# Asking for an expert's rows ahead of its weights, its gates later, and 144 idle products behind the last one

## The chip, the core and the metric

The kernel runs on one core of one Trainium2 chip. The metric is the device time of one execution in microseconds. Before the change it is 754.23 us (median of three runs, 753.93 to 754.88).

The engines as the profile names them: PE is TensorE's matmul side and PEld its weight loads, DVE is VectorE, ACT is ScalarE, POOL is GpSimd, SP issues most of the DMAs.

## The reference: attention within hash buckets, then a mixture of experts

The inputs are q, k and v of shape (4, 8, 768, 64), a projection to 6 bits, a router `w_gate` of 512 x 8 and eight experts with `w1` (512 x 1024) and `w2` (1024 x 512), all fp32. Cut to what matters:

```python
mask = q_bucket[:, :, :, None] == k_bucket[:, :, None, :]
scores = np.where(mask, scale * np.matmul(q, k.transpose(0, 1, 3, 2)), -1e9)
attn = np.exp(scores - np.max(scores, axis=-1, keepdims=True))
attn = attn / (np.sum(attn, axis=-1, keepdims=True) + 1e-09)
x = np.matmul(attn, v)                       # to (3072, 512): all heads of a token
expert_idx = np.argmax(x @ w_gate, axis=1)   # one expert a token
for e in range(E):                           # over the rows sorted by expert
    y_sorted[lo:hi] = np.maximum(x_sorted[lo:hi] @ w1[e], 0.0) @ w2[e]
out = gate_w[:, None] * y                    # rows back in their places
```

## The kernel before

**Two halves.** Up to about 450 us the attention runs over 16 pairs of heads (one batch element each four), by an order that is written out by hand. Each finished token is scattered by POOL to `sorted_rows` in DRAM: a row of 578 numbers, with its 512 features (in four pieces, each between router logits), its gate value and its token number, at a slot of its expert. Then the experts run, the most loaded first: the ranks are computed on the chip and the expert numbers read into SP's registers.

**Phases.** `PH` lists the phases: 0 and 1 are the first 256 rows and the rest of the rank-0 expert, phase n from 2 on is the expert of rank n - 1, with at most `CAPS[n - 1]` rows (512, 456, 432, ..., 354). Rows above the cap would go through a loop at the end (line 1100), which is branched around when there are none.

**Products in three parts.** An fp32 operand is split into a rounded part (fp32r) and the rest; a product is the sum of three fp32r products. So a weight goes through ACT, which copies the rounded part (L624), and POOL, which subtracts it (L625). A phase has two stages on PE: `mm1` (L729) makes eight feature blocks, 12 products each, and each block is emptied from PSUM by ACT (`relu` "u", L743) and then DVE (the rest, "d", L745); then `mm2` makes the output, for phases of at most 384 rows token by token (L786, 24 products a tile), otherwise feature by feature (L766) with transposes (L795) in the next phase. The PSUM tiles named `s` rotate over three buffers, so the fourth use of one waits for the eviction of the first. DVE scales a finished tile by its gates (L797), POOL scatters it to the output (L799).

**Weights.** A rank has four chunks: chunk 4r and 4r + 1 are the column halves of `w1`, 4r + 2 and 4r + 3 the row halves of `w2`. `raw_load(c, a)` (L611) asks for half a of chunk c, 512 KB, into rotating buffers; `chunk_part(c, i)` does a quarter of the conversion. `halves` (called after each feature block) converts a quarter and asks for a half that comes some chunks later. The buffer of a half is free when POOL has done its last quarter, and SP waits for that in its queue.

**Rows.** `rows(n)` asks SP for the rows of phase n: from phase 2 on four loads of 32-row blocks (`xb`, L641, one for each 128 features) and one small load with gate and token number (`xg`, L646). `xt_blocks(n)` later copies gate and token (L675, L657), transposes the blocks on DVE (L679) and splits them (ACT L680, DVE L682) into `xh`, which `mm1(n)` multiplies. It is called between the `mm2` tiles of phase n - 1.

**Queues.** Each engine runs its instructions in the order of the program. On ACT the conversions (L624) stand between the evictions (L743): behind feature block f stands quarter f % 4 of the next chunk, so a conversion whose weights aren't there holds back the evictions behind it. SP's DMAs all go through one queue (q1). `rows(2)` stands at the start of phase 1, behind `raw_load(4, 0)`, `raw_load(4, 1)` and `raw_load(5, 0)`.

**The end.** The last 98 rows of the last phase are made in two column halves (`youts`, L819): DVE empties the first, ACT the second (L823), POOL scatters each (L826). Then each engine branches around the loop for spilled rows (L1099) and meets the others in a barrier (L1159), ahead of which SP waits until the last output has landed.

## Time and profile before

| | before |
|---|---|
| runs | 754.23 us median (753.93 to 754.88) |
| profiled execution | 755.68 us, span 753.9 us |
| PE busy | 745.7 us (99% of the span), 4723 products |
| ACT, POOL, DVE busy | 483.2, 470.5, 456.5 us |
| DMA | 113.71 MB, 151 GB/s on average |
| phase 1 on PE | from 470.15 us (L729), its `mm2` from 481.78 us |
| phase 2 on PE | from 494.01 us |
| last product ends | 748.97 us |

In the rows of the profile a group stands as line, engine, operation, output <- input by the program's names, shapes and count; a bracket at the end of a timeline row gives the idle time of the engine ahead of it and what ended it. In a row of waits stand the total, the number and the longest, in us. "DMA to landing" is the time from a DMA's issue to its completion. An fp32 product that isn't a transpose shows as two products with a weight load each.

### The profile page before, as it was taken

The numbers are of one execution on the slowest core, as the hardware profiler recorded it, in microseconds if no ns is written. First come the engines' busy times: TensorE is split into PE (matmuls) and PEld (weight loads), VectorE is DVE, ScalarE is ACT, GpSimd is POOL, SyncE is SP. The second block draws the span as 40 slices with busy tenths as digits, with TensorE's granted clock in tenths as the row PEclk, the third lists the DMA queues.
The fourth block names the chain that finished last, engine by engine and source line by source line (L and its number), as shares of the span: only waits on it lengthen the run. The fifth ranks groups of instructions, "written<-read, shape, count | busy, mean of one in ns | idle before, by whom it ended". The sixth has DMA issues, their size and how long they took to land.

```text
span 753.9 us, 13381 instructions
## 1 busy us (share of the span) xinstructions
PE 745.7 (99%) x4723; PEld 616.2 (82%) x4723; DVE 456.5 (61%) x1042; ACT 483.2 (64%) x942; POOL 470.5 (62%) x575
## 2 busy tenths in 40 slices
PE   9999999999999999999999999999999999999997
PEld 5778777777787787877778788889999999989896
DVE  7766766767676676676688775254383925262421
ACT  7879878878887887887887761464344444453410
POOL 6867355578635768735766643576666666668532
PEclk9999999999999999999999999999999999999999
DMA  8499844235325335422343323956636476736401
GB/s 283 168 315 277 280 128 168 83 133 193 128 64 168 121 111 200 154 75 67 101 173 116 116 73 134 253 160 189 155 135 170 144 131 181 188 135 170 147 9 38
DMA packets 60181, 113.71 MB, mean 151 GB/s; under 512 B 12227, under 2 KB 27715, under 8 KB 60112
## 3 DMA queue, kind: packets, MB, share of 16 engines
q1 hardware_dynamic: 53280, 96.47, 42.3%
q0 software_dynamic: 6688, 16.35, 6.4%
q8 instruction: 38, 0.62, 0.4%
q14 instruction: 31, 0.25, 0.1%
q10 hardware_dynamic: 144, 0.02, 0.0%
HBM read 86.98 MB, written 26.33 MB: 150 GB/s over the span
## 4 chain that ended last, share of the span: by engine, by line
PE 90%; issue 3%; DMA 2%; POOL 1%; DVE 1%; ACT 1%; POOLq 0%; DVEq 0%; SPq 0%; ACTq 0%
PE t L319 17%; PE t L355 17%; PE s L729 15%; PE s L766 10%; PE s L287 9%; PE s L285 9%; PE s L786 6%; PE t L374 3%; DMA raw<-in_w1p_dram 2%; PE t L243 2%; PE s L795 1%; POOL w L625 1%; PE t L105 1%; DVE xh L682 1%; ACT e L305 0%
## 5 line engine op out<-in xcount | busy, mean ns | idle before, releaser
L295 DVE TENSOR_REDUCE m<-s 128x1 f32<-128x768 f32 x192 | 182.9, 952 | 94.8 <-PE s L287 85.6
L305 ACT ACTIVATE e<-s,m 128x768 f32<-128x768 f32 x192 | 191.2, 996 | 16.6 <-DVE m L297 9.8
L625 POOL TENSOR_TENSOR w<-raw,w 128x512 fp32r<-128x512 f32 x112 | 144.6, 1317 | 39.7 <-ACT w L624 39.1
L345 ACT ACTIVATE pt<-t 128x512 f32<-128x512 f32 (+1 forms) x253 | 142.9, 593 | 28.9 <-PE t L319 25.1
L319 PE MATMUL t<-ident,e 128*128 128x128 f32 x1152 | 160.6, 275 | 0.6 <-ACT e L305 0.4
L319 PEld LDWEIGHTS t<-ident,e 128*128 128x128 f32 x1152 | 132.6, 140 | 33.9 <-issue 12.6
L355 PE MATMUL t<-pt,vt 128*64 128x384 f32 x768 | 130.9, 490 | 0.0
L729 PE MATMUL s<-xh,w 128*128 128x456 f32 (+6 forms) x672 | 127.0, 346 | 0.7 <-DVE xh L682 0.7
L729 PEld LDWEIGHTS s<-xh,w 128*128 128x128 f32 x672 | 119.1, 188 | 4.1 <-DVE xh L682 1.0
L355 PEld LDWEIGHTS t<-pt,vt 128*64 128x64 f32 x768 | 52.2, 137 | 62.2 <-issue 60.1
L745 DVE SCALAR_TENSOR_TENSOR hh<-s,hh 128x256 fp32r<-128x256 f32 (+7 forms) x64 | 35.5, 555 | 110.8 <-ACT hh L743 109.6
L743 ACT ACTIVATE hh<-s 128x256 fp32r<-128x256 f32 (+7 forms) x64 | 31.3, 490 | 83.1 <-PE s L729 83.1
L766 PE MATMUL s<-hh,w 128*128 128x456 f32 (+3 forms) x384 | 74.9, 355 | 0.0
L624 ACT ACTIVATE w<-raw 128x512 fp32r<-128x512 f32 x112 | 66.4, 623 | 11.7 <-DMA raw<-in_w1p_dram 11.5
L766 PEld LDWEIGHTS s<-hh,w 128*128 128x128 f32 x384 | 71.1, 188 | 2.6
L799 POOL DMA_INDIRECT out_dram<-y,ix x26 | 25.9, 998 | 62.4 <-DVE y L797 37.3
L786 PE MATMUL s<-w,hh 128*128 128x512 f32 (+1 forms) x240 | 56.7, 395 | 0.8 <-ACT hh L743 0.8
L285 PE MATMUL s<-w 80*128 80x384 f32 x192 | 57.0, 378 | 0.0
L285 PE MATMUL s<-qk 80*128 80x384 f32 x192 | 56.3, 375 | 0.0
L786 PEld LDWEIGHTS s<-w,hh 128*128 128x128 f32 (+1 forms) x240 | 44.5, 187 | 11.7 <-ACT hh L743 1.3
L287 PE MATMUL s<-qk 128*128 128x384 f32 x192 | 50.0, 341 | 0.0
L253 POOL TENSOR_SCALAR bits<-bits,wsg 64x384 f32<-64x384 f32 x15 | 18.7, 1245 | 50.2 <-ACT bits L226 50.2
(202 smaller groups left out, 1018.4 us busy)
## 6 DMA issues: line engine op xcount, KB each, us to landing
raw<-in_w_dram SPq DMA_DIRECT2D x36, 512.0 KB, 3.7
raw<-in_w1p_dram SPq DMA_DIRECT2D x28, 512.0 KB, 3.8
xd<-in_qk_dram SPq DMA_DIRECT2D x16, 768.0 KB, 4.3
xhe<-in_qk_dram SPq DMA_DIRECT2D x15, 768.0 KB, 7.6
w<-in_qk_dram SPq DMA_DIRECT2D x14, 768.0 KB, 4.4
sorted_rows<-xr SPq DMA_DIRECT2D x8, 1156.0 KB, 14.5
vt<-in_v_dram SPq DMA_DIRECT2D x16, 384.0 KB, 3.9
masks<-bits SPq DMA_DIRECT2D x15, 192.0 KB, 1.9
```

The lines of the kernel that those rows point to most:

```text
L285: nc.tensor.matmul(p[:, a, :HALF], k[0:80, 2, c], k[0:80, 3, n], start=i >= 4, stop=i < 4)
L287: nc.tensor.matmul(p[:, a, :HALF], k[:, 0, c], k[:, 1, n], start=i < 4, stop=i >= 4)
L295: nc.vector.tensor_reduce(m[:, 0:1], p[:, :, :HALF], axis=AX.XY, op=OP.max)
L305: nc.scalar.activation(e, p[:, :, :HALF], AF.Exp, bias=m[:, 2:3], scale=m[:, 1:2], accum_out=SM[g, hf][:, t, s:s + 1])
L319: nc.tensor.transpose(p[:, x * 128:(x + 1) * 128], e[w][:, kt // 3, (kt % 3) * 128:(kt % 3) * 128 + 128], ident)
L345: nc.scalar.activation(o, x, AF.Copy)
L355: nc.tensor.matmul(p[s * 64:(s + 1) * 64, :HALF], VT[g][:, kt, s, :], PT[u][:, s, kt, :], start=(kt == 0), stop=(kt == NT - 1))
L624: nc.scalar.activation(w[:, 0, a], r, AF.Copy)
L625: nc.gpsimd.tensor_tensor(w[:, 1, a], r, w[:, 0, a], op=OP.subtract)
L729: nc.tensor.matmul(p[:, :c], w[:, a, d, fs], x[:, b, d, :c], start=(k == 0), stop=(k == 11))
L766: nc.tensor.matmul(p[:, :c], w[:, a, f % 4, ms], h[b][:, f, :c], start=(k == 0), stop=(k == 23))
L786: nc.tensor.matmul(p[:pw], HH[n][b][:, f, i:i + pw], w[:, a, f % 4], start=(k == 0), stop=(k == 23))
```

## The change

Three edits. `rows(2)` is called ahead of `raw_load(5, 0)`, outside of the loop, so that the four row loads of phase 2 stand ahead of the first half of chunk 5. The small load of gates and tokens is taken out of `rows` for phases from 2 on, and `row_ends(n + 1)` asks for it behind feature block 5 of phase n. And `quarters` puts 144 fp32 products behind the last one: two PSUM tiles, four strips of 32 rows of the identity (each strip writes a PSUM bank of its own) by two halves of 64 columns, 12 rounds over 96 columns and 6 over 192. Nothing reads them.

```diff
             return
...
+    def row_ends(n):
+
+        r, o, c = PH[n]
+        t = len(tiles_of(c))
+        XG[n] = P2["p"].tile([128, 4, 2], F32, name="xg", bufs=2)
+        nc.sync.dma_start(XG[n][:, :t], xsv[bass.ds(EV[r], 1), o:o + 128 * t, GC:GC + 2]
+                          .rearrange("o (j p) w -> p (o j) w", p=128))
...
+    def quarters():
+
+        x = ident[:, None, :96].to_broadcast([128, 2, 96])
+        p = [ps.tile([128, 2, 512], F32, name="s", bufs=3) for _ in range(2)]
+        for k, h in ((12, 1), (6, 2)):
+            for i in range(k):
+                for s in range(2):
+                    for a in range(4):
+                        nc.tensor.matmul(p[a // 2][64 * s:64 * s + 64, a % 2, :96 * h], ident[32 * a:32 * a + 32, :64],
+                                         x[32 * a:32 * a + 32, :h], start=(i == 0), stop=(i == k - 1))
...
+    rows(2)
     raw_load(5, 0)
     plan = spill_plan()
     for n in range(1, len(PH)):
         c0 = 4 * (PH[n][0] + 1)
         last = n + 1 == len(PH)
-        if not last:
+        if not last and n > 1:
             rows(n + 1)
         for f in range(8):
             mm1(n, f)
+            if f == 5 and not last:
+                row_ends(n + 1)
...
+    quarters()
     p2.close()
```

SP's queue at the start of phase 1, before. `raw` and `raw2` are the buffers of weight halves: the rows from `raw_5890` on are the second half of chunk 4, the two of chunk 5 and the first of chunk 6; three further row loads like the one shown are left out.

```order
L611 DMA raw_5890<-in_w1p_dram 128x2x512
...
L611 DMA raw2_5983<-in_w1p_dram 128x2x512
...
L641 DMA xb_5985<-sorted_rows 32x15x128
...
L646 DMA xg_5990<-sorted_rows 128x4x2
...
L611 DMA raw_6029<-in_w1p_dram 128x2x512
...
L611 DMA raw2_6065<-in_w2_dram 128x2x512
```

And now:

```order
L611 DMA raw_5890<-in_w1p_dram 128x2x512
...
L641 DMA xb_5983<-sorted_rows 32x15x128
...
L611 DMA raw2_5988<-in_w1p_dram 128x2x512
...
L611 DMA raw_6027<-in_w1p_dram 128x2x512
...
L611 DMA raw2_6063<-in_w2_dram 128x2x512
...
L654 DMA xg_6098<-sorted_rows 128x4x2
```

The first half of chunk 5 stands behind the four row loads, and the gates three weight halves later than they did.

PE's queue behind the last real products (L823 is the line that was L819; the waits are shown in brackets):

```order
L823 MATMUL s<-w_8269,hh_8292 98x256 x2
L823 MATMUL s<-w_8269,hh_8293 98x256
L846 MATMUL s<-ident 64x96 [waits DVE_49]
L846 MATMUL s<-ident 64x96
...
L846 MATMUL s<-ident 64x96 x93
L846 MATMUL s<-ident 64x192 x48
L1118 COMPARE_AND_BRANCH
```

Before, the branch stands right behind the L819 rows. ACT's, DVE's and POOL's queues keep their order.

## The prediction

> **What bounds the kernel now.** I read the page's head first, then the waits of PE in the expert half, then the timeline around those waits, then the tail.

> ```profile
> span 753.9 us, 13381 instructions
> PE 745.7 (99%) x4723; PEld 616.2 (82%) x4723; DVE 456.5 (61%) x1042; ACT 483.2 (64%) x942; POOL 470.5 (62%) x575
> ```

> TensorE's matmul side is busy for 745.7 of 753.9 us. Whatever neither adds products, nor opens or closes an idle spot on PE, nor touches the tail, is worth nothing. From 440 us on, PE waits twice:

> ```profile
> PE s L786 <- ACT hh L743: 0.8, 1, 0.8
> PE s L729 <- DVE xh L682: 0.7, 1, 0.7
> ```

> Both belong to the stretch that the moved loads feed. In the timeline (start, length, engine, line):

> ```profile
> 469.35 1.86 SPq L611 DMA_DIRECT2D raw<-in_w1p_dram  x3
> 475.81 2.93 SPq L646 DMA_DIRECT2D xg<-sorted_rows  x1
> 479.65 0.63 ACT L624 ACTIVATE w<-raw 128x512 fp32r<-128x512 f32 x1 [1.24 <-DMA raw<-in_w1p_dram]
> 480.19 0.37 ACT L743 ACTIVATE hh<-s 128x256 fp32r<-128x256 f32 x1
> 480.59 0.42 DVE L745 SCALAR_TENSOR_TENSOR hh<-s,hh 128x256 fp32r<-128x256 f32 x1 [1.72 <-ACT hh L743]
> 481.78 5.03 PE L786 MATMUL s<-w,hh 128*128 128x512 f32 x21
> 486.70 0.63 ACT L624 ACTIVATE w<-raw 128x512 fp32r<-128x512 f32 x1 [5.35 <-DMA raw<-in_w1p_dram]
> 487.65 6.52 PE L786 MATMUL s<-w,hh 128*128 128x512 f32 x27 [0.84 <-ACT hh L743]
> 487.97 0.74 DVE L675 COPY gate<-xg 128x4 f32<-128x4 f32 x1
> 494.01 1.61 PE L729 MATMUL s<-xh,w 128*128 128x456 f32 x7
> 496.28 18.80 PE L729 MATMUL s<-xh,w 128*128 128x456 f32 x89 [0.66 <-DVE xh L682]
> ```

> The first wait is a late weight half: ACT converts weights and empties PSUM in one queue, so when chunk 5's second half comes only at 486.7 us, the eviction of feature block 7 (behind it) and the product on it wait too. The second wait is late rows: transposing the rank-1 expert's rows starts at 487.97 and PE wants them at 495.5. In starts, 27 products of L786 take 494.01 - 487.65 = 6.36 us, 0.236 each; the first 21 took 5.87 where that pace gives 4.95: 0.9 lost. Seven of L729 took 2.27, where the pace of the 89 (0.211) gives 1.48: 0.8 lost. **1.7 us is all that PE can gain from this reordering.**

> **The change, part one: rows ahead of weights.** On SP the four row loads of the rank-1 expert (xb) now stand ahead of the first half of chunk 5 instead of behind it, and the small load of gates and tokens (xg) goes from behind the rows to behind the first half of chunk 6. No transfer is added or removed, and POOL's queue keeps its order. The landings of these rows (min/median/max after the issue), and of the two weight halves that follow them:

> ```profile
> L641 SPq DMA_DIRECT2D xb<-sorted_rows x4: 342/774/1724, 471.4 to 473.9; - x4
> DMA to landing us min/median/max: 10.5/11.3/11.5
> L611 SPq DMA_DIRECT2D raw<-in_w1p_dram x1: 1537/1537/1537, 479.0 to 479.0; - x1
> DMA to landing us min/median/max: 7.7/7.7/7.7
> L611 SPq DMA_DIRECT2D raw<-in_w_dram x1: 550/550/550, 480.7 to 480.7; - x1
> DMA to landing us min/median/max: 7.3/7.3/7.3
> ```

> The last row block lands at about 473.9 + 11.3 = 485.2 and the half asked for behind it at 479.0 + 7.7 = 486.7: what is asked first lands first. So the first half of chunk 5, ready for ACT at 479.65 now, moves behind four row blocks. If the queue is simply served in order, the pair {half, rows} ends when it ends now: the half lands at 485.2. That is the late end. The early end comes from the next expert's round, where nothing else is in flight:

> ```profile
> L641 SPq DMA_DIRECT2D xb<-sorted_rows x4: 330/332/333, 504.4 to 505.9; - x4
> DMA to landing us min/median/max: 4.2/4.5/4.8
> L611 SPq DMA_DIRECT2D raw<-in_w1p_dram x1: 768/768/768, 507.1 to 507.1; - x1
> DMA to landing us min/median/max: 6.6/6.6/6.6
> ```

> There a half behind four row blocks lands at 507.1 + 6.6 = 513.7, 9.3 us after the first row issue. Here the first row issue takes the place of the third of the three weight loads from 469.35 (about 470.8), so 480.1; one more half stands ahead than there, about 1.4 us (two halves in a row land at 486.7 and 480.7 + 7.3 = 488.0), and the blocks are somewhat larger: 482.0. Between 482.0 and 485.2 I take 483.8, nearer to the row of this very stretch, whose row blocks took more than twice as long as those of the next round.

> What is queued behind that wait: on ACT the evictions of feature blocks 5, 6 and 7. From the half's landing to a free PSUM buffer pass 481.01 - 479.65 = 1.4 us (conversion, eviction, the DVE half of it), and the first product of L786 needs that buffer. PE would start L786 at 483.8 + 1.5 = 485.3 instead of 481.78: 3.5 us. The two old stalls go: the second half, no longer behind xg's 2.93 us of issuing, comes right behind the first, some 5 us ahead of the product that needs block 7; and with PE 3.5 us later and the transposes starting no later than 488.5, the rows are ready before 497. Sum of part one: 3.5 - 1.7 = **+1.8 us**; with the ends of the landing, 0.0 (482.0) to +3.2 (485.2). Below that only a half that is not delayed at all gives the full -1.7.

> The later gates cost nothing by themselves. Worst is the last round: the load that will stand ahead of xg is issued at 693.65 and lands 6.2 us later:

> ```profile
> 693.65 9.03 SPq L611 DMA_DIRECT2D raw<-in_w_dram  x4
> DMA to landing us min/median/max: 6.2/6.2/6.2
> 700.88 0.16 DVE L675 COPY gate<-xg 128x3 f32<-128x3 f32 x1
> 716.43 5.84 PE L729 MATMUL s<-xh,w 128*128 128x354 f32 x35
> ```

> So xg is there by about 700.3, and DVE takes it at 700.88; were it late by 1 us, DVE's transposes behind it would still be 10 us ahead of their product, which starts at 716.43. The weight loads that xg lets pass are asked some 0.5 us sooner; PE never waits for them in those rounds: 0.

> **Part two: 144 idle products.** They start right behind the last real product; their PSUM buffers were emptied before. Each is 32 rows by 64 columns, fp32, so two passes, each with its weight load (the trace shows two records for each fp32 product): 288 passes. Eight (strip, column half) places get 24 passes of 96 columns and 12 of 192, 4608 columns each. The nearest rows:

> ```profile
> L355 PE MATMUL t<-pt,vt 128*64 128x384 f32 x768 | 130.9, 490 | 0.0
> L243 PE MATMUL t<-xhe,pj 128*32 128x384 f32 x120 | 12.8, 498 | 0.0
> L355 PEld LDWEIGHTS t<-pt,vt 128*64 128x64 f32 x768 | 52.2, 137 | 62.2 <-issue 60.1
> ```

> L355 runs two column halves at once: 130.9 us for 384 pairs, 0.34 us for a pass of 384 columns, 0.89 ns a column. L243 runs four column strips at once: 0.43 us a pass with its start, 1.11 ns a column. If all eight places run at once, 4608 columns are 4.1 to 5.1 us. If the four row strips take turns, four times the first: 16.4 us. No row shows row strips at once; column places do overlap in both rows, so I take 4.6 us. Its weight loads (137 ns, but half of PEld's time is hidden) fit under the streams.

> [...]

> What covers them is the wait for the last output rows:

> ```profile
> 747.75 1.22 PE L819 MATMUL s<-w,hh 128*98 128x256 f32 x9
> L1159 SPq DRAIN x3: 7/7/13, 753.0 to 753.3; - x3
> L1099 PEldq COMPARE_BRANCH x1: 363/363/363, 746.7 to 746.7; - x1
> L1099 PEldq EVENT_SEMAPHORE  x1: 51/51/51, 749.0 to 749.0; - x1
> L1099 DVEq COMPARE_BRANCH x1: 72/72/72, 746.2 to 746.2; - x1
> L1099 DVEq EVENT_SEMAPHORE  x1: 21/21/21, 746.7 to 746.7; - x1
> ```

> The last product ends at 748.97, SP's drain behind the last landing is at 753.0: 4.0 us of cover, which without the store would be none. But PE must also pass the branch around the spill loop, and its sequencer now reaches it while the idle products are nearly through. DVE needs 0.5 us from branch to the next event, PE at most 2.3 (that event waited for its last product as well). With products to 748.97 + 4.6 = 753.6, the branch about 0.3 us before that, and 0.5 to 2.3 us for it, PE arrives between 753.8 and 755.6, 0.8 to 2.6 us behind what ends the kernel now. I take the lower half: **+1.4 us**; the ends are 0 (4.1 us and a quick branch) and +2.6, +14 if strips take turns.

> **Sum.** The profiled execution took 755.68 us for its 753.9 us of span, 1.45 above the median of the runs (754.23). 755.68 + 1.8 + 1.4 = 758.9 for it, and **757.4 us** as median.

> **Rivals.** *The rows come without delaying the weights*: the half lands by about 480, both stalls vanish, the idle products stay under the store: 754.2 - 1.7 = 752.5. For it: landings of 10.5 to 11.5 us are so far above the next round's 4.5 that the rows may wait for something else than their turn, which the new order may free; against it: the landings above keep their order. *Gain and price cancel*: landing at 482.0 and a tail of 0.5: 754.8; the quick row blocks of the next round speak for it. *The row strips take turns*: 16.4 us, PE arrives 13.5 us late, 754.2 + 1.8 + 13.5 = 769.5; only L355's and L243's column overlap speaks against it. *The new stall slows PE's clock*: ten products of L105 at the start took 4.4 us, where the pace of L786 gives 2.4, so a fall costs about 2.0: 759.4.

> ```profile
> L105 PE MATMUL t<-ones 128*128 128x512 bf16 x10 | 4.4, 632 | 1.1 <-DVE warm L97 1.1
> 748.97:753.90 4.93, 0.00 (x0) 0.00 (x0) 0.00 (x0) 0.47 (x1) 0.98 (x1) 0.99 0.09 26
> ```

> Against it: in the tail PE idles for 4.93 us and the granted clock still averages 0.99, so at half it was for some 0.1 us; a stall of 3.5 us is shorter. [...]

> **How the numbers follow.** Forecast 0.50, no delay 0.13, cancel 0.20, strips in turn 0.12, clock 0.05. The forecast's own range is 755.9 (early landing, middle tail) to 760.0 (late landing, slow branch). Faster by over 0.2% (1.5 us, about what a measurement of this kernel can tell from none) holds most of the no-delay case: 0.11. Within 0.2%: the cancelling case and edges of its neighbours, 0.24. Slower: 0.65. The range for 8 in 10 goes from 752.6, into the no-delay case, to 761.0, and leaves out mostly the strips in turn.

> **What would show it.** Right: ACT's L624 on chunk 5's first half waits until 482 to 485 us, the wait of L786 moves to its first product (2 to 4 us), the waits at 486.8 and 495.6 are gone; idle products end at 753 to 754 us and PE's last events come after SP's. Wrong: L786 still begins at 481.8 (the order of asking does not set the landing), DVE waits for xg, or idle products that last beyond 6 us or end with time to spare.

## The result, and the profile after

The changed kernel takes 761.32 us (median of four, 760.70 to 762.05) against 754.56 us before (753.93 to 755.10): a ratio of 1.009, 95% interval 1.0073 to 1.0108, so +6.8 us (5.5 to 8.2). The direction is as forecast; the size is not: 757.4 us was predicted, and 761.32 lies just outside of the range. The profiled execution took 760.70 us, 5.0 more than the profiled one of before (755.68); where the other 1.8 us are is a question of its own.

The head of the changed kernel's page:

```profile
span 758.9 us, 13957 instructions
PE 751.0 (99%) x5011; PEld 621.2 (82%) x5011; DVE 457.9 (60%) x1042; ACT 482.9 (64%) x942; POOL 470.9 (62%) x575
```

The waits of PE from 440 us on (total, number, longest):

```profile
PE s L790 <- DVE hh L749: 2.8, 1, 2.8
PE s L846 <- issue: 0.9, 3, 0.4
```

Both old waits (at the second half of chunk 5 and at the rows of phase 2) are gone, and one of 2.8 us stands in their place, at the first product of phase 1's `mm2` (L790 now). The timeline of that stretch (start, length; SP's loads are grouped):

```profile
470.65 2.10 SPq L641 DMA_DIRECT2D xb<-sorted_rows  x4
472.94 3.70 SPq L611 DMA_DIRECT2D raw<-in_w1p_dram  x2
477.43 1.34 SPq L654 DMA_DIRECT2D xg<-sorted_rows  x1
483.26 0.63 ACT L624 ACTIVATE w<-raw 128x512 fp32r<-128x512 f32 x1 [5.31 <-DMA raw<-in_w1p_dram]
484.67 11.41 PE L790 MATMUL s<-w,hh 128*128 128x512 f32 x48 [2.83 <-DVE hh L749]
486.30 0.23 DVE L679 COPY gate<-xg 128x4 f32<-128x4 f32 x1
495.92 4.30 PE L733 MATMUL s<-xh,w 128*128 128x456 f32 x20
```

The first half of chunk 5 is usable (ACT's L624 takes it) at 483.26 instead of 479.65 us, 3.6 later, and PE begins `mm2` at 484.67 instead of 481.78. From there on it loses nothing, so the last real product ends at 749.9 us, 0.9 later than before. The other 4.1 us come behind it. PE's timeline from 749 us on, then the rows of lines L1118 (the branch) and L1178 (the barrier):

```profile
749.82 1.24 PE L846 MATMUL s<-ident 32*64 32x96 f32 x77
751.27 0.38 PE L846 MATMUL s<-ident 32*64 32x96 f32 x4 [0.21 <-issue]
751.98 1.93 PE L846 MATMUL s<-ident 32*64 32x96 f32 x121 [0.33 <-issue]
754.29 2.17 PE L846 MATMUL s<-ident 32*64 32x192 f32 x86 [0.38 <-issue]
```

```profile
L1118 PEldq COMPARE_BRANCH x1: 1933/1933/1933, 755.8 to 755.8; - x1
L1118 PEldq EVENT_SEMAPHORE  x1: 51/51/51, 757.8 to 757.8; - x1
```

```profile
L1178 SPq DRAIN x3: 7/7/13, 758.0 to 758.3; - x3
```

And SP's wait for PE at that barrier (total, number, longest):

```profile
SPq L1178 <- PEq L1118: 3.2, 1, 3.2
```

The idle products run from 749.82 to 756.47 us, 6.65 us with three gaps in which PE waits for nothing that the profile names; PE's branch takes 1.93 us (0.36 before), SP waits 3.2 us for PE, and it passes the output's barrier at 758.02 us where it passed at 753.01. So PE, and no longer the last store, is what the end waits for.

### The profile page after: what moved, and what is told of

Same layout as the page of the kernel before. It is cut to its first block, busy times and chain, and to the rows that moved or that the text cites. A ratio compares the mean times of both kernels' runs of the same rounds, so it can differ in the third digit from the quotient of the medians.

```text
span 758.9 us, 13957 instructions
## 1 busy us (share of the span) xinstructions
PE 751.0 (99%) x5011; PEld 621.2 (82%) x5011; DVE 457.9 (60%) x1042; ACT 482.9 (64%) x942; POOL 470.9 (62%) x575
## 4 chain that ended last, share of the span: by engine, by line
PE 96%; DMA 1%; SPq 1%; ACT 1%; issue 1%; DVE 0%; DVEq 0%; ACTq 0%
PE s L733 17%; PE t L319 17%; PE t L355 17%; PE s L770 10%; PE s L287 9%; PE s L285 9%; PE s L790 8%; PE t L374 3%; PE t L243 2%; DMA raw<-in_w1p_dram 1%; PE s L799 1%; PE s L823 1%; PE s L846 1%; PE t L105 1%; SPq L509 0%
## 5 line engine op out<-in xcount | busy, mean ns | idle before, releaser
L355 PE MATMUL t<-pt,vt 128*64 128x384 f32 x768 | 130.9, 490 | 0.0
L355 PEld LDWEIGHTS t<-pt,vt 128*64 128x64 f32 x768 | 52.2, 137 | 62.2 <-issue 60.1
L624 ACT ACTIVATE w<-raw 128x512 fp32r<-128x512 f32 x112 | 66.4, 622 | 7.4 <-DMA raw<-in_w1p_dram 7.3
L790 PE MATMUL s<-w,hh 128*128 128x512 f32 (+1 forms) x240 | 56.5, 394 | 2.8 <-DVE hh L749 2.8
L790 PEld LDWEIGHTS s<-w,hh 128*128 128x128 f32 (+1 forms) x240 | 44.6, 187 | 13.5 <-DVE hh L749 3.0
```

The costliest lines, as they stand in the source:

```text
L355: nc.tensor.matmul(p[s * 64:(s + 1) * 64, :HALF], VT[g][:, kt, s, :], PT[u][:, s, kt, :], start=(kt == 0), stop=(kt == NT - 1))
L624: nc.scalar.activation(w[:, 0, a], r, AF.Copy)
L790: nc.tensor.matmul(p[:pw], HH[n][b][:, f, i:i + pw], w[:, a, f % 4], start=(k == 0), stop=(k == 23))
```

## Experiments

All of these were timed beside the kernel before. The difference is (ratio - 1) x 754.5 us. Two more, with tiny products at the start, were timed in one execution each (758.75 and 758.24 us beside 753.46) and are read by their traces.

| kernel | ratio (95%) | difference, us |
|---|---|---|
| the change | 1.0090 (1.0073 to 1.0108) | +6.8 |
| without idle products | 1.0038 (1.0023 to 1.0053) | +2.9 |
| the same, second time | 1.0037 (1.0024 to 1.0051) | +2.8 |
| idle products only | 1.0054 (1.0037 to 1.0072) | +4.1 |
| gates later only | 1.0000 (0.9991 to 1.0009) | 0.0 |
| rows early only | 1.0043 (1.0028 to 1.0058) | +3.2 |
| two rows early, two late | 1.0016 (1.0007 to 1.0026) | +1.2 |
| rows behind both halves | 0.9997 (0.9989 to 1.0006) | -0.2 |
| without idle products, stall filled | 1.0033 (1.0020 to 1.0045) | +2.5 |
| 48 wide idle products | 1.0011 (0.9998 to 1.0024) | +0.8 |
| 144 narrow idle products | 1.0059 (1.0042 to 1.0076) | +4.5 |
| 16 idle products | 0.9993 (0.9981 to 1.0004) | -0.5 |
| 144 on one strip | 1.0359 (1.0339 to 1.0378) | +27.1 |

### The change in two halves

Without idle products (rows early, gates late):

```diff
-    quarters()
     p2.close()
```

> The change without its idle products: rows early, gates late. Theory by the two traces (the first product of the rank-0 expert's last stage waits 2.8 us, both old waits are gone, the last real product ends 0.9 us later): +0.9 us on the kernel before. The prediction's term: +1.8 us. Rival, that the part of the timed difference that the profiled executions do not show (6.8 timed against 5.0 profiled) belongs to the rows: +2.7 us.

And the idle products alone, in the kernel before:

```diff
+    quarters()
     p2.close()
```

> The kernel before with the 144 idle products alone. Theory by the traces (the products take 6.65 us instead of the predicted 4.6, the branch behind them some 2 us): +4.1 us, with the last product's end unmoved at about 749.0 and PE's last event about 757 us. The prediction's term: +1.4 us. Rival, that the unprofiled rest belongs to the tail (a longer stall of the instruction feed in most executions): +5.9 us.

The halves add up: 2.9 + 4.1 = 7.0 against 6.8. The tail comes out as its trace says, +4.1 (2.8 to 5.4). The rows do not: +2.9 (1.7 to 4.0) instead of the +0.9 that the two profiled executions show; so, by the middles of the two intervals, the 1.8 us that the profiled executions do not show belong to the rows.

### Why the tail costs 4.1 and not 1.4

Is it the columns, the instructions, or the branch? The edits here are shown against the kernel with the idle products alone. As many columns in a third of the instructions:

```diff
-        x = ident[:, None, :96].to_broadcast([128, 2, 96])
+        x = ident[:, None, :96].to_broadcast([128, 4, 96])
...
-        for k, h in ((12, 1), (6, 2)):
+        for k, h in ((6, 4),):
```

> The kernel before with 48 idle products of 384 columns in place of the 144: as many columns at each place (4608), a third of the instructions (96 passes). Theory, that the 96-column products go as fast as instructions come (16 ns a pass in the trace of the idle products alone, where the places would take 10) and that about 1 us of stalls without a waiting cause is instruction supply: the products take 4608 columns x 0.85 ns = 3.9 us without a gap, PE passes the branch some 2.6 us sooner than with 144, and the time is +1.5 us on the kernel before. Rival, that the columns set it: no change, +4.1 us.

As many instructions, 8 columns each:

```diff
-        x = ident[:, None, :96].to_broadcast([128, 2, 96])
+        x = ident[:, None, :8].to_broadcast([128, 2, 8])
...
-                        nc.tensor.matmul(p[a // 2][64 * s:64 * s + 64, a % 2, :96 * h], ident[32 * a:32 * a + 32, :64],
-                                         x[32 * a:32 * a + 32, :h], start=(i == 0), stop=(i == k - 1))
+                        nc.tensor.matmul(p[a // 2][64 * s:64 * s + 64, a % 2, :8], ident[32 * a:32 * a + 32, :64],
+                                         x[32 * a:32 * a + 32, :1], start=(i == 0), stop=(i == k - 1))
```

> The kernel before with the same 144 idle products of 8 columns each (a twelfth and less of the columns, all 288 passes). Theory of instruction supply: 288 passes x 16 ns = 4.7 us and about 1 us of stalls, so the products take 5 to 6 us and the time is +3 to +3.7 us on the kernel before. Rival, that the columns set it: 0.3 us, and no difference to the kernel before (0).

One round of each width, 16 products:

```diff
-        for k, h in ((12, 1), (6, 2)):
+        for k, h in ((1, 1), (1, 2)):
```

> The kernel before with 16 of the 144 idle products, one round of each width (32 passes). Theory: products about 0.5 us, then 2 us for the branch, so PE is through some 2.5 us behind its last real product, under the wait for the output (4 us): no difference to the kernel before (0). Rival, that any idle product behind the last one costs the end its branch time: +1 to +2 us.

The timeline of PE in the kernel with the original idle products alone:

```profile
747.32 3.30 PE L1066 MATMUL s<-ident 32*64 32x96 f32 x202
751.61 2.17 PE L1066 MATMUL s<-ident 32*64 32x192 f32 x86 [0.99 <-issue]
```

With the wide ones, and the branch there:

```profile
747.59 4.13 PE L1066 MATMUL s<-ident 32*64 32x384 f32 x96
```

```profile
L1111 PEldq COMPARE_BRANCH x1: 236/236/236, 750.5 to 750.5; - x1
```

With the narrow ones, and the branch:

```profile
748.38 2.61 PE L1066 MATMUL s<-ident 32*64 32x8 f32 x202
752.42 1.46 PE L1066 MATMUL s<-ident 32*64 32x8 f32 x86 [1.43 <-issue]
```

```profile
L1111 PEldq COMPARE_BRANCH x1: 2389/2389/2389, 753.5 to 753.5; - x1
```

And with 16:

```profile
747.88 0.75 PE L1066 MATMUL s<-ident 32*64 32x96 f32 x32
```

It is the instructions. The wide products take 4.13 us for the same 4608 columns a place, without a gap, and the branch behind them 0.24 us: +0.8, no longer told from nothing. The narrow ones, with a sixteenth of the columns, cost as much as the original: 5.5 us of products, a gap behind pass 202 and a branch of 2.4 us (their clock is at half from 752.36 us on, which is the last 86 passes and the branch). Sixteen products cost nothing and their branch takes 0.36 us, so idle products do not lengthen the branch by being there. Not all of the lost time stands in gaps: the first 202 of the original passes take 3.30 us, 16 ns each, where in undisturbed stretches eight passes of 96 columns start every 82 to 83 ns, 10 ns each; the cause of these smaller stalls is not shown. What the wide kernel's 0.8 us are stays open: in its trace the last output packet lands 3.2 us behind POOL's issue instead of 2.2, with a packet of 16 KB of instructions in that time; but such a packet runs within the same store with 16 products too, and there it lands after 2.2.

That the gap stands behind pass 202 whatever the width suggested packets of instructions: on one DMA queue (q8) 38 of 16 KB come in the kernel before, and 40 in the changed one. To tell packets from products, 20 or 60 tiny products at the very start of the program shift PE's stream by 40 or 120 instructions:

```diff
+    p = ps.tile([128, 512], F32, name="t", bufs=2)
+    for _ in range(20):
+        nc.tensor.matmul(p[:, :8], ones, ones[:, :8], start=True, stop=True)
```

> The kernel before with the 144 idle products behind the last one, and 20 tiny bf16 products (8 columns) more on PE at the very start, which move everything behind them by 40 instructions in PE's stream. In all three traces with 288 idle passes PE stands still for 1.0 to 1.4 us behind pass 202 of them, whatever their width. Theory, that it waits there for the next 16 KB of its instructions, whose bounds lie at fixed places of the stream (every 256 instructions, 128 passes): the gap comes behind pass 182, as long as before, 1.36 to 1.5 us behind the end of an instruction packet's transfer, and the branch behind the idle products waits for the packet after it. Rival, that the gap comes from the idle products themselves (so many passes into two PSUM tiles, or a full queue): it stays behind pass 202.

> The same with 60 tiny products at the start, 120 instructions. Theory of the instruction packets: the gap of 1.0 to 1.4 us comes behind pass 142, and another bound, at pass 270, comes within the idle products or just at the branch. Rival: the gap stays behind pass 202.

PE's timeline with 20, and with 60:

```profile
747.88 2.88 PE L1069 MATMUL s<-ident 32*64 32x96 f32 x182
751.93 2.35 PE L1069 MATMUL s<-ident 32*64 32x96 f32 x106 [1.17 <-issue]
```

```profile
748.40 4.81 PE L1069 MATMUL s<-ident 32*64 32x96 f32 x270
754.43 0.86 PE L1069 MATMUL s<-ident 32*64 32x192 f32 x18 [1.22 <-issue]
```

The gap moves to pass 182, and with 60 to pass 270, which is 142 + 128: with a weight load and a product to each pass, the bounds of these traces lie 256 instructions apart in the stream. At 142 there was no gap, against what was expected; in that trace the packet before had begun at 747.98, ahead of the idle products (748.40), and that it was there in time is the author's reading. In the five traces with a gap behind pass 182, 202 or 270, PE resumes 1.36 to 1.51 us behind the end of a 16 KB instruction packet (in the changed kernel the packet of 752.06 takes 0.88 us, PE resumes at 754.29). The branch of 1.9 to 2.4 us ends 1.41 or 1.42 us behind the next packet in all four traces that have one there (changed kernel: 755.39 + 0.98 + 1.41 = 757.78); with 60 tiny products no packet comes before its end, and it takes 0.38 us. The 288 passes run through more than two stretches of 256 instructions in some 6 us, where the packets of the attention came some 18 us apart (25 from 23.59 to 453.81 us in the kernel before), and at the bound PE stood idle for 1.0 to 1.4 us in four traces and for 0.38 in the changed kernel, which had lost 0.54 in two smaller gaps before. These two, between passes 77 and 82, stand in the changed kernel alone and have no packet of q8 ahead of them; their cause stays open. That PE waits for its instructions at the bounds is the author's reading of these times: the rows name no releaser there.

All products on the first row strip:

```diff
-                        nc.tensor.matmul(p[a // 2][64 * s:64 * s + 64, a % 2, :96 * h], ident[32 * a:32 * a + 32, :64],
-                                         x[32 * a:32 * a + 32, :h], start=(i == 0), stop=(i == k - 1))
+                        nc.tensor.matmul(p[a // 2][64 * s:64 * s + 64, a % 2, :96 * h], ident[:32, :64],
+                                         x[:32, :h], start=(i == 0), stop=(i == k - 1))
```

> The kernel before with the 144 idle products, all of them on the first strip of 32 rows (two column halves, four PSUM banks as before). Theory, that the four row strips run at once and that alone brings 288 passes into some 6.5 us: now four passes follow each other at each place, 96 x 82 ns + 48 x 162 ns = 15.7 us, and the time is +12.7 us on the kernel before. Rival, that strips make no difference (the pace is set by the instructions alone): +4.1 us.

By windows of PE (length, busy time, passes; granted clock; DMA):

```profile
748.40:754.20 5.80, 5.80 (x119) 1.00 0.08 24
754.20:778.00 23.80, 23.73 (x173) 0.50 0.01 1
```

The strips do run at once, or one strip would not need 29.6 us. The size was off by the clock: it falls to half at 754.2 us although PE shows no idle time. At full clock it would be 5.8 + 23.8 / 2 = 17.7 us, against the expected 15.7.

### Why the rows cost 2.9 and not 0.9

The change without idle products once more:

> The change without its idle products once more, beside its two variants of this call. +2.9 us on the kernel before as the first time; and in its profile a wait of 2.8 to 3.6 us ahead of the first product of the rank-0 expert's last stage. By the theory of the clock windows the granted clock falls behind it if 1.7 us or more of the wait lie within one window of 3.41 us.

This second profile of the change without idle products is a twin of the changed kernel's own: the half usable at 483.25 and 483.26 us, `mm2` from 484.66 and 484.67. The twin's `mm2` in the timeline:

```profile
484.66 12.96 PE L790 MATMUL s<-w,hh 128*128 128x512 f32 x48 [2.73 <-DVE hh L749]
```

Its windows (PE, PEld, DVE, ACT and POOL busy, granted clock, DMA share, GB/s), and the same of the changed kernel:

```profile
482.00:486.00 4.00, 1.34 (x4) 1.11 (x5) 1.08 (x3) 2.75 (x7) 2.05 (x2) 0.91 0.90 294
486.00:490.00 4.00, 4.00 (x13) 3.14 (x12) 3.91 (x7) 2.44 (x5) 3.00 (x4) 0.66 0.47 136
```

```profile
482.00:486.00 4.00, 1.33 (x6) 1.10 (x7) 1.07 (x3) 2.74 (x7) 2.04 (x2) 1.00 1.05 351
486.00:490.00 4.00, 4.00 (x19) 3.25 (x18) 3.81 (x7) 2.46 (x5) 3.08 (x4) 1.00 0.54 150
```

The same wait, and the same 48 products take 12.96 us instead of 11.41: the granted clock is at half from 485.27 to 488.68 us, 3.41 us, and that costs 1.55 us. The clock's changes in a trace lie whole multiples of 3.413 us apart: in the kernel before it rises at 6.28 and falls at 753.80 us, 219 of them, in the changed kernel at 5.49 and, behind the last instruction, at 759.83 us, 221. In windows of that length counted off from the changes, the idle time of PE is: twin, 2.73 us in the window that ends at 485.27, where the clock falls; first profile of the same kernel, 1.66 in one window without a fall and 1.89 in the next, at whose end (487.25) it falls; rows early only, 1.91, and it falls; the changed kernel, 1.51 and 1.32 on the two sides of a bound, and it does not. So the wait of 2.73 us, which lay in one window, came with 1.55 us more in the twin, and the one of 2.83 us, which a bound divided, with nothing in the changed kernel. The least idle time ahead of a fall is 1.89 us in these four traces and the most without one 1.66; what makes the clock fall is not shown.

Of the twelve executions of the change without idle products seven had a mean granted clock of 0.996 or 0.997 and a median of 758.22 us, five 0.999 or 1.000 and a median of 756.69: 1.5 us apart, as in the twins. In the changed kernel's four the clock is 1.000 three times and 0.998 once (762.05 us, the longest); 756.69 - 754.56 + 4.1 = 6.2 us is what the rows without a fall and the tail make together, and the three at 1.000 are 6.1 to 6.8 us above the kernel before.

Filling the wait with idle products (n == 1 is phase 1):

```diff
+    def fill():
+
+        x = ident[:, None, :].to_broadcast([128, 4, 128])
+        p = ps.tile([128, 512], F32, name="t", bufs=2)
+        for i in range(3):
+            nc.tensor.matmul(p, ident, x, start=(i == 0), stop=(i == 2))
...
             halves(c0, f)
+            if n == 1 and f == 7:
+                fill()
```

> The change without its idle products at the end, and with 3 idle fp32 products (six passes of 512 columns, by the pace of the attention's products 0.455 us each, 2.7 us) on PE ahead of the first product that waits for the late weight half. They lie within the wait (2.8 to 3.6 us in the traces of the change with and without idle products at the end) and end before it does. Theory, that in most executions the granted clock falls to half for one window of 3.4 us behind this wait (seen for 3.41 us in the profile of the change without idle products and for 6.83 us with the rows alone moved) and that this costs 1.7 us each: no fall in any execution, and the time is 1 to 1.7 us below the same kernel without the three, +1.2 to +1.9 on the kernel before. Rival, that the fall costs nothing because the weights are the bound there: the same as without them, +2.9 us.

```profile
481.94 2.73 PE L1078 MATMUL t<-ident 128*128 128x512 f32 x6
485.14 11.40 PE L790 MATMUL s<-w,hh 128*128 128x512 f32 x48 [0.46 <-DVE hh L749]
```

The fill does what it should in its trace: `mm2` takes 11.40 us at full clock. Five of its six executions lie within 756.48 and 757.12 us, where the unfilled kernel ranges from 756.09 to 759.25; the sixth is at 758.76. By the ratios it gains 0.3 us on its neighbour (2.5 against 2.8), by the medians 1.1 (756.86 against 757.95): less than expected, and the timing alone doesn't prove it. The price of a fall is shown by the twins, not by this.

The gates alone (their load is taken out of `rows` as in the change), and the rows alone (with the gates right behind them):

```diff
     raw_load(5, 0)
...
+            if f == 5 and not last:
+                row_ends(n + 1)
```

> The kernel before with only the gates and tokens asked for later; the rows stay behind the first half of chunk 5. Theory: the second half of chunk 5 no longer stands behind 2.9 us of issuing, lands some 3 us sooner, and both old waits of PE (0.8 and 0.7 us in the waits, 1.7 in starts) go: -1.7 us. If the landing is set by the rows in flight and not by the time of asking: the 0.8 us wait stays and it is 0 to -0.8. Rival, that the gates come too late for the transposes (asked at about 480, landing up to 11 us later): second wait 3 to 4 us, +2 us.

```diff
+    rows(2)
     raw_load(5, 0)
     plan = spill_plan()
...
-        if not last:
+        if not last and n > 1:
             rows(n + 1)
```

> The kernel before with only the rows ahead of the first half of chunk 5, the gates right behind the rows as before. Theory: the gates' issue (1.3 to 2.9 us) now stands ahead of the first half of chunk 5 as well, so it becomes usable for ACT at 484.6 to 486.2 instead of 483.3, and the wait of the first product of the stage grows from 2.8 to 4.1 to 5.7 us: +2.2 to +3.8 us on the kernel before. Rival, that the wait for the half is set by the row blocks in flight and not by the time of asking: as the change without idle products, +0.9.

Waits of PE with the gates alone, then `mm2` with the rows alone:

```profile
PE s L733 <- DVE xh L686: 0.3, 1, 0.3
```

```profile
485.57 14.03 PE L786 MATMUL s<-w,hh 128*128 128x512 f32 x48 [2.99 <-DVE hh L745]
```

The gates take the first old wait away and bring 0.0 us, where up to 1.7 was expected. The reason is in the other kernels whose first 740 us are those of the kernel before. Waits of PE from 440 us on, with narrow, with 16, and with the original idle products (there from 30 us on; its one wait is the gap of the tail):

```profile
PE s L729 <- DVE xh L682: 0.6, 1, 0.6
PE s L786 <- ACT hh L743: 0.4, 1, 0.4
```

```profile
PE s L729 <- DVE xh L682: 0.6, 1, 0.6
```

```profile
PE s L1066 <- issue: 1.0, 1, 1.0
```

Up to the tail, with those of the kernels with wide products (none) and one strip (0.6), that is 0, 0, 0.6, 0.6 and 1.0 us, 0.4 in the mean, where the profiled execution of before had 1.5. **Most of the old waits belong to that execution, not to the kernel**; of the 62 executions of it beside the variants 53 were shorter than its 755.68 us. In the same five traces the last real product ends at 747.39 to 748.46 us, 747.97 in the mean, where it ended at 748.97; from there the changed kernel's 749.89 is 1.9 us late, and 1.55 us for a fall in seven of twelve executions are another 0.9: 2.8 in all, as the rows measure. The shift from one baseline to the other is also the larger part of what the two profiled executions left out: before's stood 1.1 us above its median, the changed kernel's 0.6 below. The rows alone cost 3.2 us, not told from the 2.9 with the gates late: what the gates' issue adds to SP's queue is small (the half is usable at 484.16 us, not at 484.6 to 486.2; with the gates late it was at 483.25 and 484.31), and in the profile the clock stays at half for two windows (6.83 us; `mm2` 14.03 us).

Two rows ahead and two behind, and all four behind both halves:

```diff
-    rows(2)
+    rows(2, (0, 1))
     raw_load(5, 0)
+    rows(2, (2, 3))
```

> As the change without idle products, but two of the four row loads stand ahead of the first half of chunk 5 and two behind it. Theory, that each load ahead delays the half by its turn in the queue (3.6 us for four of them, so 0.9 each): the half is ready for ACT at 481.5, PE's wait shrinks from 2.8 to 3.6 us to 1.0 to 1.8, too short for the clock to fall, and the time is +0.5 to +1.2 us on the kernel before. Rival, that one load ahead brings all of the delay: +2.9 us. Rival, that the delay comes only when the last rows and the half meet: 0.

```diff
-    rows(2)
     raw_load(5, 0)
...
             halves(c0, f)
+            if n == 1 and f == 1:
+                rows(2)
```

> The other direction: the four row loads behind both halves of chunk 5 (behind feature block 1), gates late as in the change, no idle products. Theory of the order of asking: both halves land by about 484, neither weight wait of PE is left; the rows are asked for some 3 to 4 us later than before and land at about 487 to 489, so the transposes begin up to 2 us late and PE's wait for them (0 to 0.7 us in the traces so far) becomes 1 to 2.5: 0 to +2 us on the kernel before. Rival, that the rows are ready in time all the same: -0.5 us, and a version faster than both.

```profile
482.86 0.63 ACT L624 ACTIVATE w<-raw 128x512 fp32r<-128x512 f32 x1 [4.91 <-DMA raw<-in_w1p_dram]
484.28 11.38 PE L792 MATMUL s<-w,hh 128*128 128x512 f32 x48 [2.43 <-DVE hh L751]
```

```profile
495.15 5.04 PE L733 MATMUL s<-xh,w 128*128 128x456 f32 x23 [0.60 <-DVE xh L686]
```

With two rows ahead (first fence) the half is usable at 482.86 us, only 0.4 sooner than with four: the delay isn't a turn of 0.9 us for each load, and the wait of 2.4 us is beyond what was expected, although the time (+1.2) is at the upper end of it. The half was asked for at 471.62 us, ahead of the second two row loads (from 472.20), and landed 11.2 us later; these landed 11.9 to 12.4 us after their issue. So they were in flight together, and what is asked for behind the half may delay it too; what exactly does stays open. With the rows behind both halves (second fence) PE waits 0.6 us for them, as in four of the eight traces whose first 740 us are those of the kernel before, and the time is -0.2 us: no difference. None of these orders beats the kernel before.

## The prediction, step by step

- **The half's landing, right.** 483.8 predicted, with 482.0 to 485.2; usable at 483.26. `mm2` was to begin at 485.3 and began at 484.67; that four rows ahead delay the first half and the wait goes to the first product of L790 is what the profile shows.
- **"The two old stalls go: -1.7", the step that failed in part one.** They went, but most executions don't have them: the mean of the five other traces is 0.4 us by the waits. The stalls were part of why the profiled execution stood 1.45 us above the median; the sum took the gain of 1.7 from it and then the whole distance to the median as well. The delay of 3.5 was too long as well: `mm2` began 2.9 us later than in the profile of before, and 2.7 later than in the mean of the five (482.00). The two errors go opposite ways, so that the term of +1.8 comes near the +1.9 of the changed kernel's trace, without a fall of the clock, is in part luck. With the falls +2.9 (1.7 to 4.0) was measured.
- **"The new stall slows PE's clock", a rival at 0.05.** This happened, by mean clocks of 0.996 or 0.997, in seven of twelve executions without idle products, and not in the changed kernel's own profile (1.000). The price was about right (2.0 predicted, 1.55 in the twins); the argument against it failed. It read a limit on the length of a stall from the tail, but the falls behind this wait came at bounds of windows of 3.41 us, behind 1.89 us of idle time or more in one. In that tail the bounds lie at 750.38 and 753.80 us: the window up to the first holds 1.42 us of idle time, the one up to the second is idle throughout, and there the clock falls. So 4.93 us of idle time at an almost full clock say nothing of a stall of 3.5.
- **Gates later: 0, right** (0.0, -0.7 to +0.7).
- **The row strips run at once, right**: +27 us on one strip, 4.13 us for all columns on four, within the 4.1 to 5.1 that the sum had.
- **"I take 4.6" and "the lower half" of the branch, the steps that failed in part two.** The tail was +4.1 instead of +1.4, and this is the larger part of the miss. Products were priced by columns, from rows whose passes are four times as long, and the sum had no term for the number of instructions. The 144 short ones are 576 instructions in a row, more than two stretches of 256, and take 6.65 us, with the last gap ending 1.36 us behind the end of a packet; the branch behind them ends 1.41 us behind one more, at 1.93 us near the upper end of 0.5 to 2.3. Of the 2.7 us that were missing 2.05 are the products, and some 0.7 what follows them: SP passes the barrier 1.55 us behind their end, and the sum had 0.8. The signs in "What would show it" had this one: idle products beyond 6 us.
- **The sum.** For the profiled execution 758.9 was predicted, 760.70 came: 0.9 for the rows instead of 1.8, 4.1 for the tail instead of 1.4.

## What to carry to other kernels

A stall seen in one profiled execution is worth what it is in the median execution: look whether that execution is already slow by the same amount before its stall is counted as a gain. The idle products of this kernel were priced by their number, not by their work: 144 cost 4.1 us, and 4.5 with 8 columns each, where 48 with as many columns in all cost 0.8; a forecast of short instructions in a row should count them as well as their columns. And a stall of 2.73 us on PE cost this kernel another 1.55 us at half clock where it lay in one of the clock's windows of 3.413 us, one of 2.83 us nothing where a bound divided it.
